# A hand-set order on all engines, staged weight rounding, and score banks for each head, in an attention and MLP kernel

## The chip, the cores and the metric

The kernel runs on one core of one Trainium2 chip. The metric is the device time of one execution in microseconds (us). In the profile TensorE is called PE (its weight loads PEld), VectorE DVE, ScalarE ACT and GpSimd POOL. On one core there is no second die to compare with. A kernel that was timed in rounds has several runs, all of them fast ones here; a kernel that ran once has one run, whose state is unknown. A single run is therefore read through the lengths of its stages, which repeat well: the last stage is 1345.3 or 1345.4 us in seven of the nine kernels that keep ACT's new order, and within 0.6 us of that in the other two.

Ratios are computed as the mean time of one kernel's runs over that of the other's of the same rounds, so they are not quite the ratios of the medians quoted beside them.

## The reference, cut to what matters

```python
# 8 batches, 8 heads, 576 positions, head width 64, fp32, tau = 0.02
scores = scale * np.matmul(q, k.transpose(0, 1, 3, 2))
thresh = np.max(scores, axis=-1, keepdims=True) - tau
scores = np.where(scores >= thresh, scores, -1000000000.0)
scores = scores - np.max(scores, axis=-1, keepdims=True)
attn = np.exp(scores)
attn = attn / (np.sum(attn, axis=-1, keepdims=True) + 1e-09)
x = np.matmul(attn, v)            # heads side by side: 4608 x 512
h = x @ w_in                      # 512 x 2048
r = np.maximum(h, 0.0)
out = (r * r) @ w_out             # 2048 x 512
```

The two weight matrices arrive as float64. The kernel reads each number as two 32-bit words and puts the fp32 value together on chip, in 32 pieces of 128 x 512.

## The kernel before

A step is one block of 128 query rows of a pair of heads (the fifth block of a pair is 64 rows of each head together). There are 160 steps. Steps of one pair make a visit; the first visits are cut in two, so they have three and two steps. The MLP comes in twelve chunks of 384 tokens, laid as filler between the steps' matmuls; the first is available at step 13. Only TensorE's instructions stand in the order of the program. Those of DVE, ACT, GpSimd (POOL in the profile) and the DMA queue are ordered by a scheduler.

One score tile holds both heads; exp and threshold pass alternate head by head:

```python
def scores(vis, i):
    sc = psum.tile([P, 2 * n, 512], FP32, tag="sc", name="sc")
    for half in range(2):
        for u in range(n):                       # n = 2 heads, 1 in a last block
            ...
            nc.tensor.matmul(sc[:, 2 * u + half, 0:HALF], lhsT, kT[rows, at:at + HALF], ...)
    nc.vector.tensor_reduce(out=mx, in_=s, axis=AX.XY, op=ALU.max)
    ...                                          # bias, thr, z (DVE), z1 (GpSimd)
    for u in range(n):
        nc.scalar.activation(out=wu, in_=s[:, u], func=AF.Exp, bias=bias[:, u:u + 1], scale=SCALE)
        nc.vector.scalar_tensor_tensor(out=wu, in0=s[:, u], scalar=thr[:, u:u + 1], in1=wu,
                                       op0=ALU.is_ge, op1=ALU.mult, accum_out=sm[:, u:u + 1])
    ...                                          # den, rcp (DVE), normalisation (GpSimd)
```

A weight piece is rounded in one go, eight operations on three engines:

```python
def round_weights(i):
    sc = pool.tile([P, 3, WP], FP32, tag="cv", name="cv")       # two buffers
    nc.scalar.activation(out=e, in_=hi.bitcast(FP32), func=AF.Square)
    nc.gpsimd.tensor_scalar(out=t, in0=e, scalar1=2.0 ** -30, ...)
    nc.scalar.activation(out=d, in_=lo, func=AF.Copy, scale=2.0 ** -52)
    nc.vector.scalar_tensor_tensor(out=tu, in0=hi, scalar=3, in1=tu, ...)
    nc.vector.scalar_tensor_tensor(out=tu, in0=hi, scalar=0xC0000000, in1=tu, ...)
    nc.vector.tensor_scalar(out=eu, in0=tu, scalar1=0xFF800000, ...)
    nc.gpsimd.tensor_tensor(out=d, in0=d, in1=e, op=ALU.mult)
    nc.gpsimd.tensor_tensor(out=dst, in0=t, in1=d, op=ALU.add)
```

A step in the program, with some lines joined and conditions left out, and with `turn` the transposes of the block before and their copies, and `prep` the transposed queries and keys of the next visit (two on DVE, then a small key copy on GpSimd):

```python
scores(n, i)
if s in mixes: mix(*mixes[s])
fill(quarter)
for part in range(3):
    turn(*steps[s - 1], part)
    fill(quarter)
if at == 1: prep(n + 1, 0); prep(n + 1, 1)
for i in range(done, min(done + pieces[s], n_pieces)):    # 1 a step, 3 from step 12
    load_weights(i + RAW - 1); round_weights(i)
```

## Time and profile before

The median before is 1757.38 us, of the 3 runs that stood before the change was tried (1756.61 to 1758.6); with a fourth of the same rounds it is 1757.68. The page's busy times and, from its chain that ended last, the shares by engine:

```profile
PE 1570.3 (89%) x6464; PEld 847.3 (48%) x6464; DVE 693.0 (39%) x1705; ACT 575.4 (33%) x1157; POOL 610.1 (35%) x847
...
PE 79%; POOL 4%; ACT 3%; DVE 3%; issue 1%; ACTq 0%; DVEq 0%; POOLq 0%
```

TensorE is 89% busy over the whole span, and four fifths of the chain is its work. These are averages over very unlike stages. All that follows is read in four stages, whose borders are the first row-maximum reduction of step 13, 28 and 40:

| stage | what it holds | before, us |
|---|---|---|
| steps 0 to 12 | attention and weight pieces, no MLP | 183.7 |
| steps 13 to 27 | attention, most pieces, first MLP chunks | 160.2 |
| steps 28 to 39 | attention and MLP, TensorE nearly full | 100.9 |
| steps 40 to the end | TensorE-bound | 1311.5 |

### The profile page before, as it was taken

What the parts mean: (1) busy time and instruction counts of PE and PEld (TensorE: products, weight loads), DVE (VectorE), ACT (ScalarE), POOL (GpSimd) and SP (SyncE); (2) the same over time, 40 slices, a digit from 0 to 9 for tenths busy, and PEclk for the clock granted to TensorE, in tenths of its full rate; (3) what the DMA queues carried; (4) which work ended last, traced back from release to release, by engine and by line L of the source; (5) the groups of instructions that cost most, each with busy time, mean ns of one, the idle gap of its engine ahead of it and who ended that gap; (6) DMA issues with size and microseconds to landing.
All of it is one profiled execution on the core that took longest, in us unless ns stands there. A gap on an engine that the chain in (4) does not pass through costs nothing.

```text
span 1756.3 us, 18657 instructions
## 1 busy us (share of the span) xinstructions
PE 1570.3 (89%) x6464; PEld 847.3 (48%) x6464; DVE 693.0 (39%) x1705; ACT 575.4 (33%) x1157; POOL 610.1 (35%) x847
## 2 busy tenths in 40 slices
PE   2443648888999999999999999999999999999999
PEld 1222324444555555555545545545545545545453
DVE  4655555444433433433434434333434434330000
ACT  3333333333432433333333333333333324332010
POOL 5767885322422322322322312313313313312020
PEclk9566788999999999999999999999999999999999
DMA  6323433111011111111111111011111100000000
GB/s 138 85 63 92 103 79 55 27 29 38 14 27 26 21 27 33 21 24 29 21 27 33 19 29 25 16 33 27 21 30 23 21 20 13 8 12 7 12 7 18
DMA packets 224190, 59.29 MB, mean 34 GB/s; under 512 B 215392, under 2 KB 215392, under 8 KB 224096
## 3 DMA queue, kind: packets, MB, share of 16 engines
q1 hardware_dynamic: 224064, 58.10, 14.9%
q8 instruction: 51, 0.84, 0.2%
q14 instruction: 43, 0.35, 0.1%
q0 software_dynamic: 32, 0.00, 0.0%
HBM read 48.63 MB, written 9.44 MB: 33 GB/s over the span
## 4 chain that ended last, share of the span: by engine, by line
PE 79%; POOL 4%; ACT 3%; DVE 3%; issue 1%; ACTq 0%; DVEq 0%; POOLq 0%
PE o L266 27%; PE h L250 27%; PE sc L173 9%; PE x_ps L234 8%; PE w_ps L207 6%; POOL cv L108 2%; ACT w L188 2%; DVE st L178 1%; POOL w_out_sb L117 1%; DVE w L189 1%; POOL cv L116 1%; ACT wT L208 1%; POOL w L194 1%; PE w_ps L211 0%; ACT wT L214 0%
## 5 line engine op out<-in xcount | busy, mean ns | idle before, releaser
L250 PE MATMUL h<-xT,w_in_sb 128*128 128x384 f32 x1536 | 551.9, 494 | 0.0
L266 PE MATMUL o<-w_out_sb,g 128*128 128x512 f32 x1152 | 539.6, 598 | 0.0
L178 DVE TENSOR_REDUCE st<-sc 128x2 f32<-128x1152 f32 (+1 forms) x160 | 197.9, 1237 | 574.8 <-PE sc L173 574.8
L250 PEld LDWEIGHTS h<-xT,w_in_sb 128*128 128x128 f32 x1536 | 272.8, 192 | 163.6 <-issue 31.9
L194 POOL TENSOR_SCALAR w<-w,st 128x576 f32<-128x576 f32 x288 | 237.7, 834 | 317.3 <-DVE st L192 296.5
L188 ACT ACTIVATE w<-sc,st 128x576 f32<-128x576 f32 x288 | 213.5, 741 | 385.0 <-DVE st L179 293.5
L189 DVE SCALAR_TENSOR_TENSOR w<-sc,st,w 128x576 f32<-128x576 f32 x288 | 235.3, 817 | 198.9 <-ACT w L188 197.9
L266 PEld LDWEIGHTS o<-w_out_sb,g 128*128 128x128 f32 x1152 | 200.6, 190 | 189.0 <-issue 187.7
L256 POOL TENSOR_TENSOR g<-r 128x384 f32<-128x384 f32 x192 | 160.1, 834 | 351.6 <-ACT r L254 348.9
L208 ACT COPY wT<-w_ps 128x384 f32<-128x384 f32 x384 | 182.4, 477 | 278.6 <-PE w_ps L207 278.2
L173 PE MATMUL sc<-kT,qT 64*128 64x288 f32 x1024 | 175.7, 460 | 97.6 <-DVE w L189 82.1
L207 PEld LDWEIGHTS w_ps<-ident,w 128*128 128x128 f32 x1152 | 150.5, 146 | 195.7 <-issue 100.1
L207 PE MATMUL w_ps<-ident,w 128*128 128x128 f32 x1152 | 196.9, 286 | 43.1 <-ACT wT L208 25.5
L173 PEld LDWEIGHTS sc<-kT,qT 64*128 64x128 f32 x1024 | 97.4, 200 | 183.7 <-issue 136.9
L254 ACT ACTIVATE r<-h 128x384 f32<-128x384 f32 x192 | 94.1, 490 | 267.0 <-PE h L250 264.1
L234 PE MATMUL x_ps<-wT,vs 128*64 128x192 f32 (+1 forms) x1280 | 178.4, 427 | 0.0
L184 POOL TENSOR_SCALAR st<-st 128x2 f32<-128x2 f32 (+1 forms) x160 | 33.2, 208 | 359.1 <-DVE st L183 355.2
L234 PEld LDWEIGHTS x_ps<-wT,vs 128*64 128x64 f32 x1280 | 89.8, 143 | 83.1 <-issue 76.9
L108 POOL TENSOR_SCALAR cv<-cv 128x512 f32<-128x512 f32 x32 | 65.0, 2031 | 14.8 <-ACT cv L107 12.8
L173 PE MATMUL sc<-kT,qmid 128*128 128x288 f32 x128 | 40.6, 443 | 29.9 <-DVE w L189 29.9
L111 DVE SCALAR_TENSOR_TENSOR cv<-area,cv 128x512 uint32<-128x512 uint32 x32 | 22.7, 710 | 76.7 <-POOL cv L108 76.7
L116 POOL TENSOR_TENSOR cv<-cv 128x512 f32<-128x512 f32 x32 | 45.4, 1419 | 17.1 <-DVE st L191 6.2
(39 smaller groups left out, 575.5 us busy)
## 6 DMA issues: line engine op xcount, KB each, us to landing
ql<-in_q_dram SPq DMA_DIRECT2D x144, 72.0 KB, 2.4
kl<-in_k_dram SPq DMA_DIRECT2D x144, 72.0 KB, 2.5
vs<-in_v_dram SPq DMA_DIRECT2D x72, 128.0 KB, 2.3
out_dram<-osb SPq DMA_DIRECT2D x36, 256.0 KB, 2.0
area<-in_moe_w_in_dram SPq DMA_DIRECT2D x16, 512.0 KB, 5.6
area<-in_moe_w_out_dram SPq DMA_DIRECT2D x16, 512.0 KB, 4.2
vs<-in_v_dram SPq DMA_DIRECT2D x72, 16.0 KB, 2.1
ntau<-in_tau_dram POOLq DMA_DIRECT2D x1, 0.5 KB, 3.2
```

Of the source, the lines that this page charges most:

```text
L108: nc.gpsimd.tensor_scalar(out=t, in0=e, scalar1=2.0 ** -30, scalar2=2.0 - 2.0 ** -23, op0=ALU.is_ge, op1=ALU.mult)
L173: nc.tensor.matmul(sc[:, 2 * u + half, 0:HALF], lhsT, kT[rows, at:at + HALF], start=True, stop=True)
L178: nc.vector.tensor_reduce(out=mx, in_=s, axis=AX.XY, op=ALU.max)
L188: nc.scalar.activation(out=wu, in_=s[:, u], func=AF.Exp, bias=bias[:, u:u + 1], scale=SCALE)
L189: nc.vector.scalar_tensor_tensor(out=wu, in0=s[:, u], scalar=thr[:, u:u + 1], in1=wu, op0=ALU.is_ge, op1=ALU.mult, accum_out=sm[:, u:u + 1])
L194: nc.gpsimd.tensor_scalar(out=w[:, u, :], in0=w[:, u, :], scalar1=z[:, u:u + 1], scalar2=rcp[:, u:u + 1], op0=ALU.add, op1=ALU.mult)
L207: nc.tensor.transpose(ps[:, n, :], w.rearrange("p u k -> p (u k)")[:, c * P:(c + 1) * P], ident)
L208: nc.scalar.copy(wT[:, 3 * part:3 * part + 3, cols], ps[:, 0:3, :])
L234: nc.tensor.matmul(ps[u * D:(u + 1) * D, 0:nq], vs[n % 2][:, u * (NBLK + 1) + c, :], wT[:, cw, cols], start=(c == 0), stop=(c == NBLK))
L250: nc.tensor.matmul(h, w_in_sb[:, c, f * P:(f + 1) * P], xT[:, c, at:at + TCH], start=(c == 0), stop=(c == NMC - 1))
L256: nc.gpsimd.tensor_tensor(out=gs[j, f], in0=r, in1=r, op=ALU.mult)
L266: nc.tensor.matmul(o, gs[j, f][:, t * P:(t + 1) * P], w_out_sb[:, f, :], start=(f == 0), stop=(f == NFT - 1))
```

## The change

The intent is to shorten the start. A weight piece loses GpSimd's costliest operation and is split into three stages (ACT, DVE, GpSimd), each placed at its own point of the step; the first 12 steps get half a piece each. Each head gets its own pair of score banks, so that one head's banks come free while the other's are still read. The threshold passes leave `scores` and come after the second transposes. And the order of the program becomes the order of every engine. Cut to its core (cuts are marked with dots):

```diff
+MANUAL = ("PE", "DVE", "Activation", "Pool", "SP")
-    ctx.enter_context(tc.manual_schedule(engines={mybir.EngineType.PE}))
+    ctx.enter_context(tc.manual_schedule(engines={getattr(mybir.EngineType, e) for e in MANUAL}))
...
+        if stage == 0:
+            nc.scalar.activation(out=e, in_=hi.bitcast(FP32), func=AF.Copy, scale=2.0 ** -112)
+            nc.scalar.activation(out=d, in_=lo, func=AF.Copy, scale=2.0 ** -52)
+        elif stage == 1:
+            nc.vector.tensor_scalar(out=tu, in0=hi, scalar1=0x80000000, ..., op0=ALU.bitwise_and)
+            nc.vector.scalar_tensor_tensor(out=tu, in0=eu, scalar=3, in1=tu, ...)
+            nc.vector.tensor_scalar(out=eu, in0=tu, scalar1=0xFF800000, ..., op0=ALU.bitwise_and)
+        else:
+            nc.gpsimd.tensor_tensor(out=d, in0=d, in1=e, op=ALU.mult)
+            nc.gpsimd.tensor_tensor(out=weight_piece(i)[1], in0=t, in1=d, op=ALU.add)
...
-        sc = psum.tile([P, 2 * n, 512], FP32, tag="sc", name="sc")
+        sc = [psum.tile([P, 2, 512], FP32, tag=f"s{u}", name=f"s{u}") for u in range(n)]
+        halves = [(half, u) for half in range(2) for u in range(n)]
+        if early():
+            halves.sort(key=lambda x: x[1])
...
+    def threshold(vis, i):        # the passes, den, rcp and the normalisation, out of scores()
...
-    pieces = [1 if s < min(chunk_at) - 1 else 3 for s in range(NST)]
+    FEW, MORE = 0.5, 1.6
...
             scores(n, i)          # ends with the exps of both heads
+        for p in now:
+            round_weights(p, 0)
...
         for part in range(3):
             turn(*steps[s - 1], part)
+            if part == 1 and s < NST:
+                for p in now:
+                    round_weights(p, 1)
+                threshold(n, i)
             fill(quarter)
         if s < NST:
+            for p in now:
+                round_weights(p, 2)
+                if p + RAW < n_pieces:
+                    load_weights(p + RAW)
...
                 if at == 1:
                     prep(n + 1, 0)
                     prep(n + 1, 1)
```

More of the change, by code (lines that the diff above doesn't have):

```diff
@@ L95, in load_weights, with round_weights @@
         nc.sync.dma_start(out=weight_area(i).bitcast(mybir.dt.int64), in_=weight_piece(i)[0])
-    def round_weights(i):
+    rounding = {}
+    def round_weights(i, stage):
         words = weight_area(i).bitcast(U32).rearrange("p (n w) -> p n w", w=2)
         lo, hi = words[:, :, 0], words[:, :, 1]
-        dst = weight_piece(i)[1]
-        sc = pool.tile([P, 3, WP], FP32, tag="cv", name="cv")
-        t, e, d = sc[:, 0, :], sc[:, 1, :], sc[:, 2, :]
+        if stage == 0:
+            rounding[i] = pool.tile([P, 3, WP], FP32, tag="cv", name="cv")
+        t, e, d = (rounding[i][:, x, :] for x in range(3))
         tu, eu = t.bitcast(U32), e.bitcast(U32)
-        nc.scalar.activation(out=e, in_=hi.bitcast(FP32), func=AF.Square)
-        nc.gpsimd.tensor_scalar(out=t, in0=e, scalar1=2.0 ** -30, scalar2=2.0 - 2.0 ** -23,
-                                op0=ALU.is_ge, op1=ALU.mult)
-        nc.scalar.activation(out=d, in_=lo, func=AF.Copy, scale=2.0 ** -52)
-        nc.vector.scalar_tensor_tensor(out=tu, in0=hi, scalar=3, in1=tu, op0=ALU.logical_shift_left,
-                                       op1=ALU.bitwise_and)
-        nc.vector.scalar_tensor_tensor(out=tu, in0=hi, scalar=0xC0000000, in1=tu, op0=ALU.bitwise_and,
-                                       op1=ALU.bitwise_or)
-        nc.vector.tensor_scalar(out=eu, in0=tu, scalar1=0xFF800000, scalar2=None, op0=ALU.bitwise_and)
-        nc.gpsimd.tensor_tensor(out=d, in0=d, in1=e, op=ALU.mult)
-        nc.gpsimd.tensor_tensor(out=dst, in0=t, in1=d, op=ALU.add)
+        if stage == 0:
+            nc.scalar.activation(out=e, in_=hi.bitcast(FP32), func=AF.Copy, scale=2.0 ** -112)
+            nc.scalar.activation(out=d, in_=lo, func=AF.Copy, scale=2.0 ** -52)
+        elif stage == 1:
+            nc.vector.tensor_scalar(out=tu, in0=hi, scalar1=0x80000000, scalar2=None, op0=ALU.bitwise_and)
+            nc.vector.scalar_tensor_tensor(out=tu, in0=eu, scalar=3, in1=tu, op0=ALU.logical_shift_left,
+                                           op1=ALU.bitwise_or)
+            nc.vector.tensor_scalar(out=eu, in0=tu, scalar1=0xFF800000, scalar2=None, op0=ALU.bitwise_and)
+        else:
+            nc.gpsimd.tensor_tensor(out=d, in0=d, in1=e, op=ALU.mult)
+            nc.gpsimd.tensor_tensor(out=weight_piece(i)[1], in0=t, in1=d, op=ALU.add)
     loaded, ready = {}, {}
@@ L164, in scores @@
         n = 2 if i < NBLK else 1
-        sc = psum.tile([P, 2 * n, 512], FP32, tag="sc", name="sc")
-        for half in range(2):
-            for u in range(n):
-                if i < NBLK:
-                    rows, lhsT = slice(u * D, (u + 1) * D), qT[u * D:(u + 1) * D, i * P:(i + 1) * P]
-                else:
-                    rows, lhsT = slice(0, P), qmid[vis % 2]
-                at = (0 if u else REST) + half * HALF
-                nc.tensor.matmul(sc[:, 2 * u + half, 0:HALF], lhsT, kT[rows, at:at + HALF],
-                                 start=True, stop=True)
-        s = sc[:, :, 0:HALF].rearrange("p (u h) k -> p u h k", h=2)
-        st = pool.tile([P, 8, 2], FP32, tag="st", name="st", bufs=4)
-        mx, bias, thr, z, z1, sm, den, rcp = (st[:, j, 0:n] for j in range(8))
-        nc.vector.tensor_reduce(out=mx, in_=s, axis=AX.XY, op=ALU.max)
+        sc = [psum.tile([P, 2, 512], FP32, tag=f"s{u}", name=f"s{u}") for u in range(n)]
+        halves = [(half, u) for half in range(2) for u in range(n)]
+        if early():
+            halves.sort(key=lambda x: x[1])
+        for half, u in halves:
+            if i < NBLK:
+                rows, lhsT = slice(u * D, (u + 1) * D), qT[u * D:(u + 1) * D, i * P:(i + 1) * P]
+            else:
+                rows, lhsT = slice(0, P), qmid[vis % 2]
+            at = (0 if u else REST) + half * HALF
+            nc.tensor.matmul(sc[u][:, half, 0:HALF], lhsT, kT[rows, at:at + HALF], start=True, stop=True)
+        st = pool.tile([P, 7, 2], FP32, tag="st", name="st", bufs=4)
+        mx, bias, thr, z = (st[:, j, 0:n] for j in range(4))
+        for u in range(n):
+            nc.vector.tensor_reduce(out=mx[:, u:u + 1], in_=sc[u][:, :, 0:HALF], axis=AX.XY, op=ALU.max)
         nc.vector.tensor_scalar(out=bias, in0=mx, scalar1=-SCALE, scalar2=None, op0=ALU.mult)
@@ L183, in scores @@
         nc.vector.tensor_tensor(out=z, in0=thr, in1=mx, op=ALU.is_gt)
-        nc.gpsimd.tensor_scalar(out=z1, in0=z, scalar1=float(S), scalar2=1e-9, op0=ALU.mult, op1=ALU.add)
         w = pool.tile([P, n, S], FP32, tag="w", name="w", bufs=3)
         for u in range(n):
+            nc.scalar.activation(out=w[:, u, :].rearrange("p (h k) -> p h k", h=2), in_=sc[u][:, :, 0:HALF],
+                                 func=AF.Exp, bias=bias[:, u:u + 1], scale=SCALE)
+        weights[vis, i] = w, sc, st
+    def threshold(vis, i):
+        w, sc, st = weights[vis, i]
+        n = len(sc)
+        mx, bias, thr, z, sm, den, rcp = (st[:, j, 0:n] for j in range(7))
+        for u in range(n):
             wu = w[:, u, :].rearrange("p (h k) -> p h k", h=2)
-            nc.scalar.activation(out=wu, in_=s[:, u], func=AF.Exp, bias=bias[:, u:u + 1], scale=SCALE)
-            nc.vector.scalar_tensor_tensor(out=wu, in0=s[:, u], scalar=thr[:, u:u + 1], in1=wu, op0=ALU.is_ge,
-                                           op1=ALU.mult, accum_out=sm[:, u:u + 1])
-        nc.vector.tensor_tensor(out=den, in0=sm, in1=z1, op=ALU.add)
+            nc.vector.scalar_tensor_tensor(out=wu, in0=sc[u][:, :, 0:HALF], scalar=thr[:, u:u + 1], in1=wu,
+                                           op0=ALU.is_ge, op1=ALU.mult, accum_out=sm[:, u:u + 1])
+        nc.vector.scalar_tensor_tensor(out=den, in0=z, scalar=float(S), in1=sm, op0=ALU.mult, op1=ALU.add)
         nc.vector.reciprocal(rcp, den)
@@ L195, in scores @@
                                     scalar2=rcp[:, u:u + 1], op0=ALU.add, op1=ALU.mult)
-        weights[vis, i] = w
     def turn(vis, i, part):
-        w = weights[vis, i]
+        w = weights[vis, i][0]
         tag = "mm" if early() and part else "tr"
@@ L324, in fill @@
             fn(*what)
-    pieces = [1 if s < min(chunk_at) - 1 else 3 for s in range(NST)]
+    FEW, MORE = 0.5, 1.6
+    at_once = min(chunk_at) - 2
+    rounded = [min(n_pieces, int(FEW * (min(s, at_once) + 1) + MORE * max(s - at_once, 0))) for s in range(NST)]
     load_qk(0)
     load_v(0)
-    done = 0
-    for i in range(RAW - 1):
+    for i in range(RAW):
         load_weights(i)
@@ L336 @@
         state["step"] = s
+        now = range(rounded[s - 1] if s else 0, rounded[s]) if s < NST else ()
         if s < NST:
             n, i = steps[s]
-            if i == visits[n][1][0] and n + 1 < len(visits):
+            at = visits[n][1].index(i)
+            if at == 0 and n + 1 < len(visits):
                 load_qk(n + 1)
             scores(n, i)
+        for p in now:
+            round_weights(p, 0)
         if s in mixes:
@@ L350 @@
                 turn(*steps[s - 1], part)
+            if part == 1 and s < NST:
+                for p in now:
+                    round_weights(p, 1)
+                threshold(n, i)
             fill(quarter)
         if s < NST:
-            at = visits[n][1].index(i)
+            for p in now:
+                round_weights(p, 2)
+                if p + RAW < n_pieces:
+                    load_weights(p + RAW)
             if n + 1 < len(visits):
@@ L359 @@
                     load_v(n + 1)
-            for i in range(done, min(done + pieces[s], n_pieces)):
-                if i + RAW - 1 < n_pieces:
-                    load_weights(i + RAW - 1)
-                round_weights(i)
-                done += 1
 _INS = ['q', 'k', 'v', 'tau', 'moe_w_in', 'moe_w_out']
```

## The prediction

> **What bounds the kernel now.** A "step" is one block of 128 query rows for a pair of heads: scores, maximum, exp, threshold pass, normalisation, nine transposes, later a mix with the values. There are 160 steps, and twelve chunks of MLP work are laid between them. First I read the slices:
>
> ```profile
> PE   2443648888999999999999999999999999999999
> ...
> PEclk9566788999999999999999999999999999999999
> ```
>
> TensorE is full from the tenth slice to the end; whatever the change can gain lies in the first 440 us. To cut that part I took the start of each row-maximum reduction (one per step) from the trace: step 0 at 11 us, step 13 (first MLP chunk available) at 184, step 28 at 344, step 40 at 445. The windows with those borders:
>
> ```profile
> 0.00:184.00 184.00, 70.55 (x290) 42.09 (x292) 106.67 (x204) 60.38 (x107) 126.17 (x117) 0.70 0.38 90
> 184.00:344.00 160.00, 111.47 (x500) 62.83 (x497) 86.39 (x187) 58.39 (x122) 104.95 (x111) 0.88 0.32 70
> 344.00:445.00 101.00, 87.90 (x387) 45.07 (x386) 44.70 (x121) 34.94 (x69) 23.43 (x45) 0.97 0.16 32
> 445.00:1757.00 1312.00, 1300.38 (x5294) 697.31 (x5292) 455.20 (x1196) 421.69 (x860) 355.52 (x576) 1.00 0.10 21
> ```
>
> Columns: stretch, length, busy us of PE, PEld, DVE, ACT, POOL, then granted clock. The last stretch is TensorE-bound (1300 of 1312 us). The first runs 13 steps in 184 us, 14 us each, with no engine full. So it is a chain; the waits of the whole run name it:
>
> ```profile
> ACT w L188 <- DVE w L189: 49.9, 78, 2.3
> ...
> PE sc L173 <- DVE w L189: 112.0, 22, 13.0
> ```
>
> TensorE waits 112 us for one thing: the threshold pass of the step before, which frees the one score tile. The timeline of an early step shows what stands in that chain:
>
> ```profile
> 111.66 2.29 PE L173 MATMUL sc<-kT,qT 64*128 64x288 f32 x8 [9.88 <-DVE w L189]
> ...
> 113.98 1.36 DVE L178 TENSOR_REDUCE st<-sc 128x2 f32<-128x1152 f32 x1 [1.86 <-PE sc L173]
> ...
> 115.32 2.18 PE L207 MATMUL w_ps<-ident,w 128*128 128x128 f32 x9 [1.37 <-POOL w L194]
> ...
> 116.31 0.48 ACT L208 COPY wT<-w_ps 128x384 f32<-128x384 f32 x1 [5.41 <-PE w_ps L207]
> ...
> 117.97 0.75 ACT L188 ACTIVATE w<-sc,st 128x576 f32<-128x576 f32 x1
> 118.75 0.82 DVE L189 SCALAR_TENSOR_TENSOR w<-sc,st,w 128x576 f32<-128x576 f32 x1 [2.34 <-ACT w L188]
> ...
> 119.61 0.74 ACT L188 ACTIVATE w<-sc,st 128x576 f32<-128x576 f32 x1 [0.89 <-DVE w L189]
> ```
>
> The exp stands behind three copies of the previous block's transposes, which wait for its normalisation. The second exp waits for the first threshold pass, for both heads share a tile. Even this step, with no weight work on its path, takes 9.7 us; steps with weight pieces take up to 20. The groups of lines show the piece's costliest operation:
>
> ```profile
> L108 POOL TENSOR_SCALAR cv<-cv 128x512 f32<-128x512 f32 x32 | 65.0, 2031 | 14.8 <-ACT cv L107 12.8
> ```
>
> [...] eight score matmuls take 2.29 us above, after 9.88 us idle, and 1.24 us in the full stretch. [...]
>
> **The change, part by part.**
>
> Steps 0 to 12 (now 184 us). Half a piece per step instead of one, and pieces lose the 2.03 us operation. Copies stand behind both exps. I follow the loop from the end of head 0's threshold pass, which now frees head 0's banks alone. [...] DVE meanwhile does the second pass and small ops (0.82+0.08+0.16+0.17 = 1.3). Reductions of one head (0.756, from the single-head row) then end at 2.95, as the second waits for scores ending at 2.2. Bias 0.2, exp 0.75, pass 0.9: the loop is 4.9 us. Every third step has a mix (3.4) and transposes (1.3) on TensorE behind 2.2 of scores: 6.9. A piece's three DVE operations (0.69+0.69+0.42 = 1.8) lie before the passes, where DVE idles 0.55: +1.25 in every second step. Average (6.9 + 2 x (4.9+0.6))/3 = 6.1[...]. TensorE is then busy 70% with gaps under 2 us, so I take it as warm. The second step starts near 16 us; 12 x 6.3 more puts step 13 at 92 us, a gain of 92.
>
> Steps 13 to 27 (now 160 us). Here come 1.6 pieces per step, in steps of one or two, with two scratch buffers. A third piece's ACT stage waits for POOL to finish the one two before, POOL's stage stands behind the normalisation, that behind the threshold pass, and that (in DVE order) behind this step's piece. It is a closed loop. For two pieces after two: POOL 2 x 2 x 1.25, ACT 1.2, DVE 1.55 (first masks overlap), passes and den 2.25, normalisation 1.65, squares 0.6: 12.2 us; with one piece on either side one POOL stage less, 9.7; a single-head step 1.6 less. From the kernel's own rounding rule: three transitions of the first kind, the rest of the second, five single-head: 9.8 on average. In visits of two steps the key copy (POOL) stands behind the pieces: some 8 us in all. 15 x 9.9 + 8 = 157 us, as good as no change, though TensorE alone needs some 6.6 per step. Step 28 falls at 249.
>
> Steps 28 to 39 (now 101 us). No pieces. TensorE work is 6.5 us per step. But the first transpose group's copy now stands behind both exps: these end 3.0 us after the scores, the copy at 3.55, and the single transpose buffer is free only then. With 0.8 us of filler per gap I get 7.2 for plain steps, up to 8.9 with a mix, 7.6 on average: 91 us. Step 40 at 340.
>
> Steps 40 to the end (now 1312 us). TensorE's work is the same. The same late copy costs where filler between scores and second group is short. Walking the kernel's filling rule with 1.29 us per h part, 1.72 per o part, 0.47 per transpose group, I count 38 of 120 steps that come early, by 1.0 us on average: 35 to 40 us given back. The GpSimd op on z1 (0.2 us x 160) vanishes off the path: nothing. So 1347.
>
> Sum: 92 + 157 + 91 + 1347 = 1687 us, 4% less.
>
> **Rivals.**
> 1. TensorE stays cold in the first steps. [...] I get 8.5 to 9 us per step: step 13 at 118 and 1713 in all. For it: PEclk 5 to 7 there. Against: those gaps are 4 to 10 us, mine under 2.
> 2. The late copy costs nothing (PE queue and filler absorb it): 1650. For it: now only 2.4 us of such waits in 440 to 1000 us. Against: now the copy slips between the exps, at 705.30 of 704.68 to 707.04, and TensorE takes it 0.05 us after.
> 3. The weight loop doesn't close (ACT and POOL drift a step apart) and steps 13 to 27 are TensorE-bound, 105 us: 1635. [...]
> 4. Steady stages lose as much as the start gains: in-order engines stall TensorE 0.9 us in every one of 120 steps. 1757, no change. Against: steps with a mix or with o parts have the slack.
>
> **Range and chances.** I give the first stage +-15 us, the weight stage +-25, the late copies +-20; independent, that is 35 us, about 45 for 8 in 10. I round to 1635 to 1730. Faster by over 2% is under 1722: 0.80; within 2% 0.17; slower 0.03.
>
> **What would show it.** Right: step 13 near 92 us with granted clock above 0.9; between 92 and 249 ACT waiting on GpSimd's last rounding stage, DVE on ACT's; at the end transposes on TensorE waiting for ACT's copy, 35 us or more, where there are 2.4 now. Wrong, if step 13 comes after 115 us, if TensorE is over 90% busy between steps 13 and 28, or if the last 120 steps take under 1320 us.

The sum came to 92 + 157 + 91 + 1347 = 1687 us. Two terms of its first stage are cut: 1.1 us a head for the score matmuls when sorted by head (2.2 for both, hence "scores ending at 2.2"), and 0.2 us a step for signals between engines, which made 12 steps of 6.1 into 12 of 6.3. Both were estimates and not shown. Rival 1 has lost the terms of its 8.5 to 9 us, and rival 3 a second way, to 1720 us. "Warm" and "cold" stand for full and half granted clock: the eight score matmuls that took 2.29 us ran at 0.50 (111.60 to 114.00), and such a group took 1.24 at 701.47, at 1.00. That gaps under 2 us would keep the array warm was an assumption.

## The result, and the profile after

The changed kernel takes 1742.35 us, the median of 4 runs (1740.16 to 1744.08), against 1757.68 before in the same rounds. The ratio is 0.9912 (95%: 0.9895 to 0.993): the same within 2%. The prediction of 1687 us was 55 too low, outside its range. By stages, read as before, with x14 (an experiment further down) in the last column:

| stage | before | predicted | after | x14 |
|---|---|---|---|---|
| steps 0 to 12 | 183.7 | 92 | 107.7 | 99.7 |
| steps 13 to 27 | 160.2 | 157 | 184.8 | 152.7 |
| steps 28 to 39 | 100.9 | 91 | 102.4 | 92.5 |
| steps 40 to the end | 1311.5 | 1347 | 1345.3 | 1307.3 |

The first stage gained 76 us. Then the second gave back 25, the third 1.5 and the last 34. The page's busy times, and TensorE's slices with the granted clock:

```profile
PE 1586.0 (91%) x6464; PEld 853.6 (49%) x6464; DVE 697.3 (40%) x1833; ACT 565.8 (33%) x1157; POOL 496.5 (29%) x655
...
PE   5766677889999999999999999999999999999999
...
PEclk8778888999999999999999999999999999999999
```

GpSimd's work fell from 610 to 497 us. The ramp of the first ten slices is steeper than before, but slices 3 to 7 stay at 6 or 7 tenths, and the clock stays at 7 or 8 up to the seventh slice, so the array was not warm at the start, as the prediction had taken it to be. (Even these means are too high: the trace has no clock record before 28.99 us, and the profile counts that time as full clock, though the score matmuls before it take 0.68 us each, as from 52.79 on, where the clock is 0.50, and not 0.40, as at 45.79, where it is 1.00.) The four stages as windows, in the columns that the prediction explains:

```profile
0.00:108.00 108.00, 68.47 (x278) 43.42 (x280) 72.74 (x176) 42.16 (x80) 40.38 (x56) 0.79 0.45 101
108.00:293.00 185.00, 125.84 (x512) 69.38 (x509) 117.70 (x235) 72.08 (x146) 101.84 (x110) 0.84 0.35 89
293.00:395.00 102.00, 87.12 (x384) 44.64 (x383) 45.03 (x131) 35.43 (x71) 22.38 (x31) 0.97 0.12 26
395.00:1740.00 1345.00, 1304.62 (x5294) 696.16 (x5293) 461.81 (x1294) 416.08 (x860) 331.88 (x459) 1.00 0.10 22
```

In the second window no engine is full: TensorE 126, DVE 118, GpSimd 102 of 185 us. It is a chain again. In the last, TensorE has the 1300 us of work it had and 40 us of gaps in place of 12. TensorE's own waits in that last stage, first before (445 to 1757), then after (395 to 1740); the columns are us in total, how often, and the longest:

```profile
PE w_ps L207 <- ACT wT L208: 6.2, 9, 1.2
```

```profile
PE w_ps L220 <- ACT wT L221: 22.5, 27, 1.4
PE w_ps L230 <- ACT wT L227: 13.6, 13, 1.4
```

The second group of transposes waits for ACT to copy the first group out of the single transpose buffer: 40 waits of 36.1 us together, where there were 9 of 6.2. One of them, on TensorE and then on ACT (start and length in us, engine, line and operation; in brackets how long the engine was idle before it, and for whom):

```profile
914.66 1.46 PE L263 MATMUL h<-xT,w_in_sb 128*128 128x384 f32 x4
916.95 0.55 PE L220 MATMUL w_ps<-ident,w 128*128 128x128 f32 x3 [0.83 <-ACT wT L221]
```

```profile
914.78 1.37 ACT L191 ACTIVATE w<-s,st 128x576 f32<-128x576 f32 x2 [3.66 <-DVE st L184]
916.04 0.49 ACT L267 ACTIVATE r<-h 128x384 f32<-128x384 f32 x1
916.41 0.49 ACT L221 COPY wT<-w_ps 128x384 f32<-128x384 f32 x1
```

ACT was idle for 3.66 us, because the exp at the head of its queue waited for the bias. Then both exps and a relu run, and only then the copy. TensorE stands for 0.83 us.

In the weight stage TensorE waits longer for those copies, too, and two waits grow that are not of this kind, before (184 to 344) and after (108 to 293):

```profile
PE sc L173 <- DVE kT L149: 4.7, 1, 4.7
PE sc L173 <- POOL kT L152: 2.2, 2, 1.4
```

```profile
PE w_ps L220 <- ACT wT L221: 30.7, 13, 5.3
PE s L179 <- POOL kT L157: 16.2, 4, 6.2
...
PE s L179 <- DVE kT L154: 4.7, 3, 2.8
```

The first score matmuls of a visit wait for its keys. The end of one two-step visit shows what the keys stand behind, on DVE, on GpSimd and on TensorE:

```profile
188.45 1.48 DVE L116 TENSOR_SCALAR cv<-area 128x512 uint32<-128x512 uint32 x1 [2.60 <-POOL w_in_sb L122]
...
192.50 0.81 DVE L203 SCALAR_TENSOR_TENSOR w<-s,st,w 128x576 f32<-128x576 f32 x1
...
194.42 0.73 DVE L154 STREAM_TRANSPOSE kT<-kl 128x576 f32<-128x576 f32 x1
```

```profile
194.67 1.26 POOL L121 TENSOR_TENSOR cv<-cv 128x512 f32<-128x512 f32 x1
196.01 1.26 POOL L122 TENSOR_TENSOR w_out_sb<-cv 128x512 f32<-128x512 f32 x1
...
197.68 0.24 POOL L157 COPY kT<-kT 64x64 f32<-64x64 f32 x1
```

```profile
195.21 0.75 PE L179 MATMUL s<-kT,qT 64*128 64x288 f32 x2 [2.75 <-DVE kT L154]
197.97 2.28 PE L179 MATMUL s<-kT,qT 64*128 64x288 f32 x6 [2.01 <-POOL kT L157]
```

DVE runs the piece, then the threshold pass, then the next visit's transposes. GpSimd runs the piece's last stage and only then the key copy of 0.24 us. TensorE waits for 2.75 us, runs one matmul (the trace records each matmul here twice) and waits for 2.01 more.

In the first stage, an early pair of steps shows a warm and a cold one, on TensorE and on DVE:

```profile
45.79 1.25 PE L179 MATMUL s<-kT,qT 64*128 64x288 f32 x8
...
52.79 2.99 PE L179 MATMUL s<-kT,qT 64*128 64x288 f32 x8 [4.61 <-DVE w L203]
55.71 2.18 PE L220 MATMUL w_ps<-ident,w 128*128 128x128 f32 x9
59.07 3.00 PE L179 MATMUL s<-kT,qT 64*128 64x288 f32 x8 [1.18 <-DVE w L203]
```

```profile
50.75 0.69 DVE L117 SCALAR_TENSOR_TENSOR cv<-cv 128x512 uint32<-128x512 uint32 x1 [1.40 <-ACT cv L113]
...
51.82 0.81 DVE L203 SCALAR_TENSOR_TENSOR w<-s,st,w 128x576 f32<-128x576 f32 x1
```

The same score group takes 1.25 us at 45.79, after a mix, at a granted clock of 1.00, and 2.99 or 3.00 afterwards, at 0.51 and 0.50. (Nine transposes take 1.20 us at 44.66, at 1.00, and 2.18 at 55.71, at 0.50.) Of the twelve groups of steps 1 to 12, eight take about 3.0, two 1.25 and two 1.95. Not all of the difference is the clock: where TensorE waits for the passes, head 1's banks come free one pass after head 0's, some 0.7 us later. With one tile for both heads (x19, below) a cold group takes 2.30 and a warm one 1.25; with own banks it is 2.99 and 1.94. By both differences the clock is worth an estimated 1.05 us a group. Two more things are to be seen. At 55.71 the transposes follow the scores without a gap, 5.1 us of unbroken work, and after only 1.18 us of idling the next group is cold all the same. And the pass at 51.82 comes late: ACT had started the exps at 48.80, two in 1.37 us, so head 0's was done near 49.5. DVE stood for 1.40 us in front of a weight piece instead, whose ACT stage runs behind both exps.

### The profile page after: what moved, and what is told of

It is laid out like the page before. It is cut to its first block, busy times and chain, and to the rows that moved or that the text cites. A ratio compares the mean times of both kernels' runs of the same rounds, so it can differ in the third digit from the quotient of the medians.

```text
span 1740.2 us, 18567 instructions
## 1 busy us (share of the span) xinstructions
PE 1586.0 (91%) x6464; PEld 853.6 (49%) x6464; DVE 697.3 (40%) x1833; ACT 565.8 (33%) x1157; POOL 496.5 (29%) x655
## 4 chain that ended last, share of the span: by engine, by line
PE 79%; DVE 8%; ACT 7%; POOL 3%; issue 2%; SPq 0%; DMA 0%; ACTq 0%; DVEq 0%; POOLq 0%
PE o L279 27%; PE h L263 24%; PE s L179 11%; PE x_ps L247 9%; PE w_ps L220 7%; DVE st L183 5%; ACT w L191 3%; ACT wT L221 1%; DVE w L203 1%; POOL cv L121 1%; DVE cv L117 1%; DVE st L184 1%; ACT cv L113 1%; ACT wT L227 1%; POOL w_in_sb L122 1%
## 5 line engine op out<-in xcount | busy, mean ns | idle before, releaser
L183 DVE TENSOR_REDUCE st<-s 128x1 f32<-128x576 f32 x288 | 207.2, 753 | 733.4 <-PE s L179 733.3
L191 ACT ACTIVATE w<-s,st 128x576 f32<-128x576 f32 x288 | 199.2, 737 | 552.0 <-DVE st L184 444.4
L203 DVE SCALAR_TENSOR_TENSOR w<-s,st,w 128x576 f32<-128x576 f32 x288 | 225.0, 814 | 79.6 <-ACT w L191 79.6
L179 PE MATMUL s<-kT,qT 64*128 64x288 f32 x1024 | 184.6, 459 | 56.9 <-DVE w L203 27.4
L179 PEld LDWEIGHTS s<-kT,qT 64*128 64x128 f32 x1024 | 104.5, 200 | 146.1 <-issue 94.9
L283 ACT COPY osb<-o 128x512 f32<-128x512 f32 x36 | 21.1, 586 | 85.3 <-PE o L279 83.5
L250 ACT COPY xT<-x_ps 128x384 f32<-128x384 f32 (+1 forms) x64 | 25.4, 397 | 51.4 <-PE x_ps L247 51.4
L179 PE MATMUL s<-kT,qmid 128*128 128x288 f32 x128 | 38.4, 425 | 3.1 <-DVE w L203 3.1
L121 POOL TENSOR_TENSOR cv<-cv 128x512 f32<-128x512 f32 x32 | 40.5, 1267 | 0.0
L188 DVE TENSOR_TENSOR st<-st 128x2 f32<-128x2 f32 (+1 forms) x160 | 38.1, 238 | 5.5
```

The source lines that it names most:

```text
L179: nc.tensor.matmul(sc[u][:, half, 0:HALF], lhsT, kT[rows, at:at + HALF], start=True, stop=True)
L183: nc.vector.tensor_reduce(out=mx[:, u:u + 1], in_=sc[u][:, :, 0:HALF], axis=AX.XY, op=ALU.max)
L191: nc.scalar.activation(out=w[:, u, :].rearrange("p (h k) -> p h k", h=2), in_=sc[u][:, :, 0:HALF], func=AF.Exp, bias=bias[:, u:u + 1], sca ...
L203: nc.vector.scalar_tensor_tensor(out=wu, in0=sc[u][:, :, 0:HALF], scalar=thr[:, u:u + 1], in1=wu, op0=ALU.is_ge, op1=ALU.mult, accum_out=s ...
```

## The experiments

Four theories stood at the start, one for each loss. **Copy:** ACT's order (exps ahead of the copy) costs the last stage. **Pass:** DVE's order (piece ahead of the threshold pass) lengthens the loop of a step. **Keys:** the next visit's transposes and key copy stand behind the pieces. **Buffers**, rival to the last two: the loop of the weight stage is closed by the two scratch buffers. For the first stage, **clock** (the array stays cold) and **overlap** (score matmuls sorted by head take longer than in pairs of heads) were rivals to pass. All kernels here give correct results.

### Is it ACT's order that costs the last stage? (x1, x8, x17)

x1 puts the first transposes' copy ahead of the exps, in steps without weight pieces:

```diff
-            scores(n, i)              # with the exps at its end
+            scores(n, i)              # without
+        copy_first = s < NST and not now and s > at_once
+        if s < NST and not copy_first:
+            exps(n, i)
...
             turn(*steps[s - 1], part)
+            if part == 0 and copy_first:
+                exps(n, i)
```

> The changed kernel, but from step 29 on the first transpose copy stands ahead of both exps on ScalarE. Theory 1 (the late copy stalls TensorE): the stretch from step 40 to the end falls from 1345 us to 1312 to 1320, waits of TensorE's transposes for ScalarE's copies there fall from some 37 us to under 10, the whole from 1742 to 1705 to 1718. Rival (the 33 us come from DVE's or GpSimd's hand order, or from the split reductions): the stretch stays above 1335 and the whole within 5 us of 1742.

Measured: 1700.37 us, ratio 0.9672 (0.9655 to 0.9688). The stages are 109.1, 185.0, 96.5 and 1307.2. The last is 38 us shorter than in the changed kernel, and TensorE's waits in it are

```profile
PE w_ps L224 <- ACT wT L225: 5.3, 9, 0.6
```

This is 9 waits of 5.3 us, nearly what the kernel before had. The copy theory holds for the last stage, and the third stage gains 6 of the 11 us by which it was over the prediction.

x8 does the same in the weight stage, too (`copy_first = s < NST and not early()`), with the pieces' ACT stage moved behind the second transposes' copy.

> From step 13 on ScalarE does the first transpose copy, then the exps, then the second copy, then the weight piece. Theory 2 (in the weight stage, too, it is the copy behind exps and pieces that holds TensorE, not the two scratch buffers): steps 13 to 28 take 148 to 168 us in place of 185, the whole 1668 to 1685. Rival (DVE[...] is full there): 175 us or more, the whole 1690 or more.

Measured: 1712.25 us, ratio 0.9738 (0.9724 to 0.9753), 12 us worse than x1. Its weight stage took 196.5 us where x1 took 185.0. The piece now starts later on ACT, and DVE still runs it ahead of the threshold pass, so the pass comes later still: DVE's waits in front of a piece for its ACT stage rose from 7.1 to 39.8 us there, and score matmuls wait 27.5 us for the pass, where they had waited for none. (Their waits for the copies fell from 38.4 to 5.3.) The expected 148 to 168 us were missed. An order that is right on one engine is wrong as long as the next engine's is.

x17, run later, has the other two repairs below (pass and prep first), but the copy ahead of the exps only from step 29.

> The three moves, but the copy goes ahead of the exps only from step 29 on. If the copy matters in the weight stage once the other two links are gone: steps 13 to 28 take 8 to 20 us more than with all three; if not (as the first two runs with it said), within 4 us.

Measured: 1661.59 us, ratio 0.9449 (0.9434 to 0.9463), 8 us behind x14, which has it everywhere. Of these the profiled run, itself the fastest of the four, shows 5.4: 1.4 in the weight stage and 3.6 in steps 28 to 39. Once the pass no longer stands behind the piece, copy first is a small gain in the weight stage and not a loss.

### Is it DVE's order? (x3, x9)

x3 lets the threshold pass go ahead of the piece's DVE stage, and changes nothing else:

```diff
             if part == 1 and s < NST:
+                threshold(n, i)
                 for p in now:
                     round_weights(p, 1)
-                threshold(n, i)
```

> The changed kernel with the threshold pass ahead of the piece's DVE operations, two buffers as before. Theory 1 (the loop is closed by DVE's order too): steps 13 to 28 take 145 to 168 us in place of 185, the first 13 steps 4 to 8 us less than 108. Rival [...]: 175 us or more in the weight stage.

Measured: 1721.95 us in one run. Stages: 99.7, 174.8, 100.4, 1345.3; the weight stage is nearer to the rival's 175 than to the expected 145 to 168. The pass behind the piece costs 8 us in the first stage, 10 in the weight stage, 2 in the third and none where no pieces are. Both changes together, x9 (x8 and x3):

> The same, and the threshold pass ahead of the piece's DVE operations. If both links hold separately: step 13 at 99 to 102 us, weight stage 138 to 158, the whole 1650 to 1670. If DVE is full in the weight stage the order of its work gives no more than 5 us there.

Measured: 1677.21 us, ratio 0.9538 (0.9522 to 0.9554). Stages: 99.9, 175.8, 92.6, 1307.3. The weight stage falls from x8's 196.5 to 175.8, which is twice what the pass alone gained in x3, but short of the 138 to 158 expected: a link was still missing.

### Do the scratch buffers close the loop? (x2, x15)

x2 gives the pieces four scratch buffers instead of two. The third part of each is now the piece's own place in the weights:

```diff
-            rounding[i] = pool.tile([P, 3, WP], FP32, tag="cv", name="cv")
-        t, e, d = (rounding[i][:, x, :] for x in range(3))
+            rounding[i] = pool.tile([P, 2, WP], FP32, tag="cv", name="cv", bufs=4)
+        t, e = (rounding[i][:, x, :] for x in range(2))
+        d = weight_piece(i)[1]
```

> The changed kernel with four scratch buffers for a weight piece in place of two (the third part of the scratch is kept in the weight tile itself[...]). Theory 1 (a closed loop through the two buffers): steps 13 to 28 take 120 to 150 us in place of 185, the whole 1685 to 1715. Rival ([...]DVE is simply full): 172 to 185 us, the whole above 1730.

Measured: 1736.01 us, ratio 0.9878 (0.9863 to 0.9892). The weight stage takes 180.8 us, 4 less. x15 is the same edit on x14:

> All three moves and four scratch buffers. If the loop through the two buffers is the next link: steps 13 to 28 take 125 to 146 us in place of 153 and the whole 1628 to 1647. If it never was one: 150 to 155 us and the whole within 3 us of 1653.

Measured: 1653.74 us, ratio 0.9405 (0.9389 to 0.9421), against x14's 1653.13: nothing. The loop through the buffers, on which the prediction's sum for this stage was built, was not what held the stage.

### Is it the next visit's keys? (x13)

x13 moves the next visit's transposes and key copy ahead of the piece's DVE and GpSimd stages, and so ahead of the threshold pass too, from step 13 on:

```diff
+            if part == 1 and s < NST and at == 1 and n + 1 < len(visits) and (not early()):
+                prep(n + 1, 0)
+                prep(n + 1, 1)
             if part == 1 and s < NST:
                 for p in now:
                     round_weights(p, 1)
...
-                if at == 1:
+                if at == 1 and not (not early()):
                     prep(n + 1, 0)
                     prep(n + 1, 1)
```

> The changed kernel, but from step 13 on the next visit's query and key transposes (VectorE) and key copies (GpSimd) stand ahead of the weight piece's operations. Theory 3 (the four ends of visits in steps 13 to 20, 66 us where I had reckoned some 42, are what the weight stage costs over the prediction): steps 13 to 28 take 155 to 170 us in place of 185, waits of the scores for key copies fall from 16 us to under 4, the whole 1712 to 1728. Rival (the pieces themselves hold the stage wherever these small operations stand): 178 us or more, the whole above 1734.

Measured: 1723.97 us, ratio 0.9808 (0.9791 to 0.9824), which leaves it open whether it is 2% faster. The weight stage takes 164.7 us, 20 less. The only wait of a score matmul that is left in it:

```profile
PE s L179 <- DVE w L203: 1.2, 2, 0.9
```

No score matmul waits for keys any more (20.9 us in the changed kernel). The four visits' last steps, from one step's first reduction to the next one's, took 65.7 us together in the changed kernel and 38.6 here. Of these 27 us, 7 came back in the other steps.

### All three orders together (x14)

> All three moves: first copy ahead of the exps, threshold pass ahead of the piece, next visit's transposes ahead of the piece. If the links add up: weight stage 140 to 158 us, step 13 at 100, from step 40 on 1307, the whole 1642 to 1662. If they are one link seen thrice: the weight stage stays at 165 to 176 and the whole at 1665 to 1677.

Measured: 1653.13 us, the median of 4 runs (1652.73 to 1653.98), ratio 0.9403 (0.9389 to 0.9417). Stages: 99.7, 152.7, 92.5, 1307.3. This is faster than both kernels, and 6% faster than the one before. The three repairs alone had gained 42, 20 and 18 us (x1, x3, x13), which adds up to 81. The kernel that has just these three is x17, and it gained 81: they simply add up, and none takes another's place. x14's 89 has the copy first in the weight stage as well. The window of its weight stage, and the two costliest of DVE's groups there:

```profile
100.00:252.00 152.00, 117.99 (x504) 66.40 (x500) 133.21 (x234) 71.15 (x146) 110.49 (x109) 0.86 0.46 110
```

```profile
L117 DVE SCALAR_TENSOR_TENSOR cv<-cv 128x512 uint32<-128x512 uint32 x24 | 29.5, 1228 | 2.9 <-ACT wT L225 0.5
L119 DVE TENSOR_SCALAR cv<-cv 128x512 uint32<-128x512 uint32 x24 | 25.5, 1061 | 0.8
```

DVE is now busy for 133 of 152 us. Much of that is longer operations: the or-operation (L117) takes 1.23 us on the mean where it took 0.69 at 50.75 above, and the mask (L119) 1.06, where the same operation took 0.43 in the early steps. In the changed kernel's trace GpSimd was idle during the or-operation at 50.75, and at work through the whole of the one at 190.03, which took 1.58. No run here took such an overlap away, so it is not shown that it is the cause, nor how much of the stage it costs.

### What holds the first stage? (x4, x10, x20, x21, x16)

x4 takes the head-sorted order of the score matmuls back (the two lines with `halves.sort` removed).

> The changed kernel with the early score matmuls in pairs of heads again. Theory 1 (TensorE is cold there and its score time stands on the loop, but the first head's reduction starts sooner when sorted): eight matmuls take 2.3 us in place of 3.0 and step 13 comes at 106 to 114 us (108 now). Rival [...]: step 13 at 98 to 103 us.

Measured: 1742.17 us in one run; first stage 108.2. A cold group still takes 2.99 us and a warm one 1.24, as 1.25 when sorted. The overlap theory falls: sorted by head, the matmuls take TensorE no longer. Nor does pairing bring back the 2.3 us that was expected, as head 1's banks come free later in either order.

x10 lays five transposes of the identity, which nobody reads, behind the real ones of each early step, to keep the array warm.

```diff
+        if early() and s > 0:
+            junk = psum.tile([P, TCH], FP32, tag="x", name="junk")
+            for _ in range(5):
+                nc.tensor.transpose(junk[:, 0:P], ident, ident)
```

> The changed kernel with five needless transposes of the identity at the end of each of the first 13 steps, where TensorE idles. Theory (those steps are longer than predicted for the clock that TensorE is granted there): eight score matmuls take 2.0 to 2.3 us in place of 3.0, and step 13 comes at 97 to 102 us in place of 108. Rival (the loop is held by DVE, or the clock doesn't follow): 106 us or later.

Measured: 1744.19 us in one run; first stage 108.9; six of the twelve score groups still at about 3.0 us and a seventh at 2.85. This left the clock theory undecided, since the array had hardly warmed (a mean granted clock of 0.81 in that stage, against 0.79). x20 therefore tries four true matmuls instead (`nc.tensor.matmul(junk[:, 0:P], ident, ident, start=True, stop=True)`).

> The changed kernel with four needless matmuls of the identity (not transposes) in each gap of the first 13 steps. Theory ([...]the half clock costs 1.1 us in each cold step): at most three of twelve score groups take 2.9 us or more, in place of eight, and step 13 comes at 97 to 103 us in place of 108. First rival (the clock is not what costs): groups under 2 us, but step 13 at 105 us or later. Second rival (the gaps are too short to change the clock): groups as now.

Measured: 1738.63 us in one run; first stage 102.3 with a mean granted clock of 0.91 (x10: 0.81, the changed kernel: 0.79; 0.80, 0.72 and 0.66, if the time before the first clock record is counted as half). Only three of the twelve groups still take about 3.0 us. Five groups more are warm than in the changed kernel, and the stage is 5.4 us shorter, 1.1 us each, about the 1.05 us found above. So a cold array does cost the changed kernel's first stage time: 5.4 us for these five groups, and by that figure an estimated 8 for all eight.

That x10's filler was transposes does not explain why it warmed so little. In x10 TensorE ran nothing but transposes, real ones and filler, from 102.46 to 105.64 us, at half clock (0.50), and the full clock (1.00) came directly after:

```profile
102.39 2.18 PE L220 MATMUL w_ps<-ident,w 128*128 128x128 f32 x9
104.37 1.27 PE L377 MATMUL junk<-ident 128*128 128x128 f32 x5
```

```profile
102.90:106.30 3.40, 2.74 (x13) 2.34 (x11) 2.93 (x6) 2.65 (x5) 1.89 (x2) 0.50 0.89 134
106.40:109.70 3.30, 2.05 (x10) 1.17 (x12) 2.94 (x9) 0.87 (x3) 0.88 (x2) 1.00 0.53 164
```

In the changed kernel, too, the very sequence that stayed cold at 59.07 (scores, nine transposes, a short gap) was followed by a warm group, at a granted clock of 1.00, when it began at 23.83:

```profile
30.02 1.94 PE L179 MATMUL s<-kT,qT 64*128 64x288 f32 x8 [1.08 <-DVE w L203]
```

What the traces show is when the clock changes: in the changed kernel at 28.99, 32.41, 42.65, 52.88 and 63.12 us, which is 3.42, 10.24, 10.23 and 10.24 us apart. Two stretches as long as the shortest of these were full of work. From 25.58 to 28.99 it was two thirds transposes, and the clock was 1.00 after it; from 52.88 to 56.29 it was 2.90 us of scores, and the clock stayed at 0.50. Why is not shown. The two fillers also differ in length (at their shortest 1.06 us of matmuls against 0.71 of transposes), and no run made them equal.

x21 is the same filler on x14:

> The three moves with the same four matmuls. Theory: step 13 at 92 to 96 us in place of 100 and the whole 1645 to 1649 in place of 1653. Rivals: step 13 at 98 us or later, the whole 1651 or more.

Measured: 1653.01 us, ratio 0.9405 (0.939 to 0.9421), against 1653.13 without. First stage 99.7 as before, although its clock rose from 0.79 to 0.90 (from 0.69 to 0.79, if the time before the first clock record is counted as half). With the pass ahead of the piece, the score matmuls' clock no longer sets the pace. Between 18 and 100 us DVE is busy for 71 of 82 us there.

x16 tests a side theory: that DVE's tiny comparison z, which took up to 1.18 us beside GpSimd's work (the changed kernel, 57.01) and 0.16 with GpSimd idle (48.85), delays the pass. It is x14 with z moved behind the passes.

> The same, and the comparison for z moved behind the threshold passes, where it is first needed. Theory [...]: step 13 at 94 to 98 us in place of 100. Rival (another operation of the chain then waits as long): within 1.5 us of the run without the move.

Measured: 1653.98 us in one run; first stage 99.6. The theory falls; where the time goes instead is not shown.

### What are the parts of the change worth? (x5, x18, x19)

x5 keeps everything but the hand order of DVE, ACT, GpSimd and the DMA queue (`MANUAL = ("PE",)`).

> The changed kernel with only TensorE in hand order, the rest left to the scheduler as before: everything of the change but the hand order. Theory (hand order gives the late copy and frees the exps early): from step 40 on 1310 to 1318 us as before the change; step 13 at 125 to 150 us; the whole 1700 to 1735. Rival (the gain at the start comes from fewer pieces and from the heads' own banks): step 13 at 105 to 115 us.

Measured: 1689.06 us, ratio 0.9604 (0.959 to 0.9619). Stages: 113.2, 145.6, 97.2, 1331.8. So the hand order alone costs 53 us: it gains 5.5 in the first stage and loses 39, 5 and 13.5 in the others. The rest of the change is worth 4% by itself, and x5 happens to come out at the predicted total, but with quite other stages. One expectation was missed: its last stage was to be 1310 to 1318 us, and took 1331.8, with 26 waits of 22.3 us for late copies, under the scheduler's order too. So of the 34 us lost there, 13.5 go with the hand order and 20 with the rest of the change; ACT's order in x1 takes both away. The weight stage of x5:

```profile
113.00:259.00 146.00, 114.30 (x510) 64.54 (x510) 107.56 (x230) 69.52 (x142) 103.90 (x107) 0.90 0.44 109
```

The same GpSimd work (104 against 102 us) and less DVE work (108 against 118) fit into 146 us instead of 185.

x18 takes the thinning back as far as possible: one piece a step at first and two later. The old three a step can't be had with this order, by reasoning and not by a run: the third stage of a step's pieces comes after the second of all of them, and with two scratch buffers a third piece would wait for ever.

```diff
-    FEW, MORE = 0.5, 1.6
+    FEW, MORE = 1, 2
```

> The changed kernel with one piece in each of the first steps and two in each later one, in place of a half and 1.6. Theory (in the first 13 steps a piece costs the 1.25 us by which its VectorE work exceeds that engine's gap, and no more): six more pieces, step 13 at 114 to 120 us in place of 108. Rival (the thinning is what made the first stage short): step 13 beyond 130 us.

Measured: 1746.25 us in one run. Stages: 119.6, 181.6, 98.0, 1345.0. Thinner pieces gain 12 us early and give 8 back later.

x19 puts both heads into one tile of four banks again:

```diff
-        sc = [psum.tile([P, 2, 512], FP32, tag=f"s{u}", name=f"s{u}") for u in range(n)]
+        both = psum.tile([P, 2 * n, 512], FP32, tag="sc", name="sc")
+        sc = [both[:, 2 * u:2 * u + 2, :] for u in range(n)]
```

> The changed kernel with one score tile of four banks for both heads. Theory (own banks let the first head's next scores start one pass, 0.9 us, earlier): step 13 at 116 to 126 us in place of 108; from step 40 on within 3 us of 1345. Rival (the scores wait for TensorE or for the transposes anyway): step 13 at 107 to 111.

Measured: 1760.04 us in one run. Stages: 118.8, 188.5, 105.0, 1345.9. Own banks are worth 11 us in the first stage, 4 in the second, 3 in the third, and nothing where TensorE is full. A cold score group takes 2.30 us here, as head 1's matmuls need not wait for a later pass, and a warm one 1.25.

## Why the prediction was wrong, point by point

The total was too low by 53 us of span: 16 in the first stage, 28 in the second, 11 in the third, and 2 the other way in the last. None of the signs that it named as fatal came true (step 13 came at 107.7 us, TensorE was 68% busy in the weight stage, the last 120 steps took 1345): the errors were terms of the sum. Of its signs of being right, the copy waits came (36.1 us), the granted clock above 0.9 did not (0.79).

**Steps 40 to the end: right.** Predicted were 38 late copies of 1.0 us and 1347 us. The trace has 40 waits of 36.1 us and 1345.3. x1 undoes it by ACT's order alone. Rival 2 (the late copy costs nothing) is refuted, and rival 4, a steady loss as large as the gain, was half true: 34 us.

**Steps 13 to 27: this is the largest error, 28 us.** The step that failed is the sentence "In visits of two steps the key copy (POOL) stands behind the pieces: some 8 us in all." The mechanism was right and the size wrong. By my sum the four steps that end these visits would have taken some 42 us; they took 65.7, while the other eleven took 119 against some 115. x13 removes the wait and 20 us of the stage with it. What I had missed is that the keys stand behind the pieces twice, on DVE first and then on GpSimd, and that the whole next step hangs on them. The rest of that sum, the closed loop through two scratch buffers, gave a plausible number by luck: with twice the buffers (x2) the stage shortens by 4 us only, and in x14 by none (x15). Of the two signs that the prediction gave for its loop, ACT waited for GpSimd's last stage for 10.5 us in all and DVE for ACT's for 7.1: both are there, both small beside 185. The order of pass and piece is worth 10 more (x3). The stage took 12.3 us a step, and x13 and x3 take 20 and 10 us off it by order alone.

**Steps 0 to 12: predicted 92, measured 107.7.** The second step came at 18.1 instead of 16, and a step took 7.5 us instead of 6.3. Two terms were off, and they aren't a sum, for they stand beside each other in one loop. First, "+1.25 in every second step" for a piece: at 49 to 52 us the pass came 2.3 us later than head 0's exp allowed, since DVE waited for the piece's ACT stage. x3 shows 8 us for it. Second, "I take it as warm": eight of twelve groups were cold, and x20 shows 5.4 us for five of them. The argument, "gaps under 2 us", fails first: before seven of the twelve groups TensorE idled for 2.7 to 4.6 us. And it isn't enough, as the group at 59.07 was cold after a gap of 1.18. Rival 1 named this, and it was partly right in cause though not in size (118 us). With pass first, warm or not, the stage is 99.7 us; the 8 us that are left over the prediction, 2 of them ahead of the second step, were not separated. And one fear of the prediction was groundless: that score matmuls sorted by head take longer (x4: 2.99 cold and 1.24 warm in pairs, 2.99 and 1.25 sorted).

**Steps 28 to 39: predicted 91, measured 102.4.** I took 7.6 us a step on the mean where it was 8.5. The copy behind the exps, which I had put at part of this, costs 6 us (x1), and the other two orders, still felt from the pieces' last steps, bring it to 92.5 in x14. Which of its terms was too low is not shown.

**Two sums and two readings that don't hold.** 6.9 and twice 5.5 average 6.0, not 6.1, and the items of the loop give 4.8, not 4.9; in the weight stage three of 12.2, twelve of 9.7 and five times 1.6 less average 9.7, not 9.8, and the product then has 9.9. Put right, the two stages would have been predicted at about 90 and 153 us, further from what was measured; the argument stays the same. TensorE is over 90% busy from the eleventh slice on, not the tenth. And the step shown "with no weight work on its path" has some: GpSimd ran the last two operations of a piece until 114.44 us, 2.3 us after the reciprocal that the normalisation needed was there, and transposes, copies and exp stood behind that.

**Where the expected gain went.** The first stage became 76 us shorter, as intended. Of these, 34 were given back in the last stage to ACT's order, hand-set or the scheduler's, and 25 in the weight stage, where x3 and x13 name DVE's and GpSimd's. All of it was ordering: x14 has the same operations, banks and pieces, and takes 1653 us. Against the scheduler's order (x5) the hand order as it was cost 53 us, and set as in x14 it gains 36.

## What to carry to other kernels

When a program's order becomes an engine's order, look for each engine at what its longest-waiting instruction holds up: work that another engine needs soon (a copy that frees a single buffer, a pass that frees banks, the next visit's keys) belongs ahead of anything that waits or that nobody awaits, and this has to be right on all engines at once, as x8 shows. A late order costs little per step and is paid in every step of the long stage: 0.9 us in every third step was 36 us of waiting here. And before filling gaps to keep an engine's clock up, see whether the path runs through that engine at all: from x14 to x21 the granted clock of the first stage rose from 0.79 to 0.90, and the stage stayed at 99.7 us.
